# A weights' loader that moves at fixed feature blocks of each token tile, in a kernel of attention and two MLPs

## The chip, the cores and the metric

The kernel runs on one core of one Trainium2 chip. The metric is the device time of one execution in microseconds (us). The kernel before took 1242.02 us (median of 3 runs, 1241.17 to 1243.66).

## The reference

Attention with a learned relative position bias (4 batches, 8 heads, 576 positions, 64 channels a head) gives 2304 tokens of 512 channels. Two MLPs follow, all in float32:

```
x = attention(q, k, v, bias).reshape(2304, 512)
h = x @ w_in                                   # 512 -> 2048
x = (h * clip(h + 3, 0, 6) / 6) @ w_out        # 2048 -> 512
gate = 1 / (1 + exp(-(x @ w_gate)))            # 512 -> 1536
return (gate * (x @ w_val)) @ w_out2           # 1536 -> 512
```

## The kernel before

Bias and attention take the first 361 us or so; the change does not touch them. What follows is called the first part (the first MLP) and the second part (the gated one).

**Tiles and blocks.** The tokens go in 6 token tiles of 384 (TW). The first part walks over its 16 feature blocks of 128 in two halves: eight blocks for all six tiles, then the other eight for all six. The second part does the same with 12 blocks, six a half. "Tile 1" to "tile 12" of a part below are these passes in order; f (first part) and e (second part) are the feature blocks. Float32 products are taken as pairs of high and low parts: a projection of one block is 12 matmuls (L507 to L509), the output projection of one block is 12 matmuls in the first part (L564: high, high, low of the activations) and 9 in the second (L619).

**The chain of a block.** First part: project into PSUM, ScalarE Relu (L513), VectorE product g (L514), ScalarE rounds g to its high part gh (L544), VectorE subtracts for the low part gl (L545), and out1 (L564) uses both two blocks later. Second part: two projections, ScalarE Sigmoid (L633), VectorE product (L634), the same split L544 and L545, and out2 (L619) one block later. At the end of a tile split_x splits the next tile's tokens (ScalarE L499, VectorE L500), and the last blocks' out1 or out2 runs; their blocks' chain is then not covered by projections of the same tile. Sums are taken out of PSUM (L307 on ScalarE, L309 or L602 on VectorE) and stored.

**The loader.** The weights come as 68 tiles of 512 columns in 8-byte numbers that must be turned into float32 and split. One tick() moves three weight tiles on by one stage each: split of tile i-2 (ScalarE cast L149, GpSimd subtraction L150), assemble of tile i-1 (VectorE L139, L141, L143), the DMAs of tiles i and i+1 (SyncE's queue, L125), magnitude of tile i (ScalarE Abs L131, VectorE L132). 28 slots hold finished tiles; a slot comes free when its block's last tile is done. go_on() ticks if a slot is free, and a loop ahead of each block ticks until that block's own weights are there (`while load.done < 2 * f + 2`). In the first part go_on is called at even blocks, and at every block of the first and the last tile of each half; in the second part at every block.

**What sets the order.** The engines run their instructions in the order of their own queues. The tile framework's scheduler sets that order: it does not keep the order of the program text, so a tick's VectorE instructions can stand some blocks away from the place of the call. Nothing in the kernel keeps them out of the last blocks of a tile.

Of the kernel before, what the change touches and what calls it, by code (L numbers as in the profile page):

```python
# [10 lines left out]
F32 = mybir.dt.float32  # L11
F32R = mybir.dt.float32r
I32 = mybir.dt.int32
AF = mybir.ActivationFunctionType
ALU = mybir.AluOpType
# [12 lines left out]
NTILE = NT // TW  # L28
# [65 lines left out]
def block_kernel(ctx: ExitStack, tc: tile.TileContext, q, k, v, mlp, w_in, w_out, w_gate, w_val, w_out2, dist_d,  # L94
                 rows_d, out):
    nc = tc.nc
# [6 lines left out]
    half = keep.tile([P, 1], F32, name="half")  # L103
# [68 lines left out]
    def ring(name):  # L172

        if name == "z":
            return stg.tile([P, 512], F32, name="z", bufs=4)
        return stg.tile([P, 2, 512], F32, name="raw", bufs=2)
# [128 lines left out]
    def evac(eng, dst, src):  # L305
        if eng == "A":
            nc.scalar.copy(dst, src)  # L307
        else:
            nc.vector.tensor_copy(dst, src)  # L309
# [106 lines left out]
    with ExitStack():  # L416
# [55 lines left out]
        pend = None  # L472
        for G in range(S // 16):
# [16 lines left out]
            pend = (G, ps)  # L490
# [6 lines left out]
        def split_x(x):  # L497
            for c in range(4):
                nc.scalar.copy(XH[:, c], x[c])  # L499
                nc.vector.tensor_tensor(out=XL[:, c], in0=x[c], in1=XH[:, c].bitcast(F32), op=ALU.subtract)  # L500

        def project(slot, ps=None):
            ps = mp.tile([P, 512], F32, name="h", bufs=4) if ps is None else ps
            for c in range(4):
                wh = slot[:, 0, P * c : P * c + P]
                wl = slot[:, 1, P * c : P * c + P]
                nc.tensor.matmul(ps[:, 0:TW], wh, XH[:, c], start=(c == 0), stop=False)  # L507
                nc.tensor.matmul(ps[:, 0:TW], wl, XH[:, c], start=False, stop=False)  # L508
                nc.tensor.matmul(ps[:, 0:TW], wh, XL[:, c], start=False, stop=(c == 3))  # L509
            return ps[:, 0:TW]  # L510

        def hardswish(g, ph):
            nc.scalar.activation(g, ph, AF.Relu, bias=half, scale=1.0 / 6.0)  # L513
            nc.vector.scalar_tensor_tensor(out=g, in0=g, scalar=1.0, in1=ph, op0=ALU.min, op1=ALU.mult)  # L514
            return g
# [5 lines left out]
        for i in range(NSLOT):  # L521
# [5 lines left out]
            if i in (NS // 2 + 1, NS // 2 + 2):  # L527
                f = len(begun)
# [9 lines left out]
        mp = ctx.enter_context(tc.tile_pool(name="mp", bufs=1, space=PSUM, reuse_waits="tile"))  # L538
        slots += [moe.tile([P, 2, 512], F32R, name=f"slot{i}") for i in range(NPRE, NALL)]

        def split_g(g):
            gh = moe.tile([P, TW], F32R, name="gh", bufs=3)
            gl = moe.tile([P, TW], F32R, name="gl", bufs=3)
            nc.scalar.copy(gh, g)  # L544
            nc.vector.tensor_tensor(out=gl, in0=g, in1=gh.bitcast(F32), op=ALU.subtract)  # L545
            return gh, gl

        def go_on(freed, to):

            if load.n - 2 < min(NALL + freed, to):  # L550
                load.tick()

        def take(src):
            x = moe.tile([P, 4, TW], F32, name="take", bufs=2)
            nc.sync.dma_start(x, src)
            return x


        def out1(f, g, os, first, last):
            gh, gl = g  # L560
            sl = slots[(2 * f + 1) % NALL]
            for r, x in ((0, gh), (1, gh), (0, gl)):
                for c in range(4):
                    nc.tensor.matmul(os[c][:, 0:TW], sl[:, r, P * c : P * c + P], x,  # L564
                                     start=(first and r == 0 and x is gh), stop=(last and x is gl))

        NH = NF // 2
        todo = [(part2, t) for part2 in range(2) for t in range(NTILE)]
        X2 = None
        for part2, t in todo:  # L570
            os, pend = [], []
            part = take(part_d[t]) if part2 else None
            for f in range(NH * part2, NH * part2 + NH):
                while load.done < 2 * f + 2:
                    load.tick()
                g = begun.pop(f) if f in begun and t == 0 else None
                if g is None:
                    g = hardswish(moe.tile([P, TW], F32, name="g", bufs=2), project(slots[2 * f % NALL]))
                if not os:
                    os += [mp.tile([P, 512], F32, name=f"o{c}") for c in range(4)]  # L580
                pend.append((f, split_g(g), os, f == NH * part2, f == NH * part2 + NH - 1))
                if len(pend) > 2:
                    out1(*pend.pop(0))
                freed = 2 * NH * part2
                if t == NTILE - 1:
                    freed += max(0, 2 * (f - NH * part2 - 1))
                if f % 2 == 0 or t == 0 or t == NTILE - 1:
                    go_on(freed, 68)
            if (part2, t) != todo[-1]:
                u = todo[todo.index((part2, t)) + 1][1]  # L590
                split_x([x[:, TW * u : TW * (u + 1)] for x in x1])
            else:
                X2 = take(x2[0])
                split_x([X2[:, c] for c in range(4)])
                X2 = take(x2[1])
            for args in pend:
                out1(*args)
            for c in range(4):
                if c % 2 == 0:
                    two = ring("raw")  # L600
                if part2:
                    nc.vector.tensor_tensor(out=two[:, c % 2, 0:TW], in0=os[c][:, 0:TW], in1=part[:, c], op=ALU.add)  # L602
                else:
                    evac("AV"[c % 2], two[:, c % 2, 0:TW], os[c][:, 0:TW])
                if c % 2 == 1:
                    nc.sync.dma_start((x2 if part2 else part_d)[t][:, c - 1 : c + 1], two[:, :, 0:TW])
# [7 lines left out]
        def out2(e, g, os, first, end, last):  # L614
            gh, gl = g
            sl = slots[(2 * NF + 3 * e + 2) % NALL]
            mm = [(i, x, r) for x, r in ((gh, 0), (gh, 1), (gl, 0)) for i in range(NB)]
            for i, x, r in sorted(mm, key=lambda m: m[0]) if last else mm:
                nc.tensor.matmul(os[i], x[:, P * i : P * i + P], sl[:, r], start=(first and x is gh and r == 0),  # L619
                                 stop=(end and x is gl))  # L620

        NH = NE // 2
        for j, (part2, t) in enumerate(todo):
            os = [mp.tile([P, 512], F32, name=f"o{c}") for c in range(NB)]
            prev = None
            for e in range(NH * part2, NH * part2 + NH):
                while load.done < 2 * NF + 3 * e + 3:
                    load.tick()
                s0 = 2 * NF + 3 * e
                pg = project(slots[s0 % NALL])  # L630
                pv = project(slots[(s0 + 1) % NALL])
                g = moe.tile([P, TW], F32, name="g", bufs=2)
                nc.scalar.activation(g, pg, AF.Sigmoid)  # L633
                nc.vector.tensor_tensor(out=g, in0=g, in1=pv, op=ALU.mult)  # L634
                gg = split_g(g)
                if prev is not None:
                    out2(e - 1, prev, os, e - 1 == NH * part2, False, False)
                prev = gg
                freed = 2 * NF + 3 * NH * part2
                if t == NTILE - 1:  # L640
                    freed += 3 * (e - NH * part2)
                go_on(freed, 68)
            if j + 1 < len(todo):
                split_x([X2[:, c] for c in range(4)])
                if j + 2 < len(todo):
                    X2 = take(x2[todo[j + 2][1]])
            out2(NH * part2 + NH - 1, prev, os, False, True, j == len(todo) - 1)
            for i in range(NB):
                o = acc[NB * t + i]
                if part2:  # L650
                    nc.vector.tensor_tensor(out=o, in0=o, in1=os[i], op=ALU.add)
                    nc.sync.dma_start(out[TW * t + P * i : TW * t + P * i + P, :], o)
                else:
                    evac("AV"[i % 2], o, os[i])
# [27 lines left out]
```

## Time and profile before

| | before |
|---|---|
| median of 3 runs | 1242.02 us |
| profiled execution: time / span | 1240.27 / 1238.5 us |
| granted TensorE clock, mean | 0.992 |
| TensorE busy | 1197.9 us (97%) |
| VectorE busy | 705.5 us (57%) |
| ScalarE busy | 557.5 us (45%) |
| GpSimd busy | 274.8 us (22%) |
| loader's DMAs (raw) | 68 of 512 KB, 3.5 us from issue to landing |
| L150 (GpSimd, loader) | 68 of 1352 ns |
| L545 (VectorE, gl) | 166 of 623 ns |
| L141, L143 (VectorE, loader) | 68 of 961 ns, 68 of 759 ns |

The span is the profiled execution from its first to its last instruction, and 1.77 us of that execution lie around it. TensorE is busy in nearly all of it, so a change can only win where TensorE waits or where its clock is not granted in full. A mean over the span hides that: the clock of 0.992 is made of long stretches at 1.0 and a few short ones well below.

### The profile page before, as it was taken

Reading aid. Unit: us, or ns where it says so; the run is one execution under the profiler, and the core shown is the slowest. Engines: PE = TensorE matmul, PEld = TensorE weight load, DVE = VectorE, ACT = ScalarE, POOL = GpSimd, SP = SyncE. Lnnn points to the kernel's source line nnn. Section 1 sums busy time; section 2 is a strip of 40 time slices with the busy share of each in tenths; the row PEclk is TensorE's granted clock in tenths of the full one; section 3 lists DMA queues with packets and bytes.
Section 4 is the critical chain, followed back from the end, with each engine's and each line's share of the span. In section 5 each row is a group of like instructions: output and inputs, shape, how many; then the busy total and the mean of one; then the engine's idle time right before and its main releaser. Section 6 shows DMA issues by size and latency. Waiting matters only on the chain.

```text
span 1238.5 us, 18871 instructions
## 1 busy us (share of the span) xinstructions
PE 1197.9 (97%) x7302; PEld 1065.0 (86%) x7302; DVE 705.5 (57%) x1402; ACT 557.5 (45%) x1171; POOL 274.8 (22%) x222
## 2 busy tenths in 40 slices
PE   7899999999998999998999999989999999999998
PEld 3367777776788999998999999979999999999998
DVE  8977787777868765367753338772212532223332
ACT  5878777777754444345433335332212432212221
POOL 4935556655412210031200003210000210000000
PEclk9999999999999999999999999999999999999999
DMA  5652636254213331032411104540000101011000
GB/s 169 231 183 79 200 88 183 87 154 115 90 35 115 118 109 60 26 128 95 152 53 52 44 28 137 175 145 26 26 1 26 60 26 52 4 47 52 26 26 26
DMA packets 36154, 106.78 MB, mean 86 GB/s; under 512 B 3936, under 2 KB 10336, under 8 KB 36064
## 3 DMA queue, kind: packets, MB, share of 16 engines
q1 hardware_dynamic: 36064, 105.57, 26.3%
q8 instruction: 57, 0.93, 0.3%
q14 instruction: 33, 0.27, 0.1%
HBM read 80.78 MB, written 24.77 MB: 85 GB/s over the span
## 4 chain that ended last, share of the span: by engine, by line
PE 79%; DVE 11%; ACT 4%; DMA 3%; issue 3%; POOL 0%; DVEq 0%; ACTq 0%; SPq 0%; POOLq 0%
PE o L564 12%; PE h L509 11%; PE h L507 11%; PE h L508 11%; PE o L619 11%; PE s L259 6%; PE av L349 5%; PE tr L317 4%; DVE z L141 2%; PE s L486 2%; PE av L352 2%; DMA raw<-in_part_dram 1%; DVE z L143 1%; DVE x L481 1%; DVE z L132 1%
## 5 line engine op out<-in xcount | busy, mean ns | idle before, releaser
L507 PE MATMUL h<-early,slot 128*128 128x384 f32 x952 | 319.0, 335 | 0.0
L509 PE MATMUL h<-early,slot 128*128 128x384 f32 x952 | 318.8, 335 | 0.0
L508 PE MATMUL h<-early,slot 128*128 128x384 f32 x952 | 318.4, 334 | 0.0
L150 POOL TENSOR_TENSOR slot<-z,slot 128x512 fp32r<-128x512 f32 x68 | 91.9, 1352 | 617.7 <-ACT slot L149 352.3
L507 PEld LDWEIGHTS h<-early,slot 128*128 128x128 f32 x952 | 179.2, 188 | 2.7
L508 PEld LDWEIGHTS h<-early,slot 128*128 128x128 f32 x952 | 178.8, 188 | 2.6
L509 PEld LDWEIGHTS h<-early,slot 128*128 128x128 f32 x952 | 178.6, 188 | 0.0
L544 ACT CAST gh<-g 128x384 fp32r<-128x384 f32 x166 | 85.1, 513 | 185.9 <-DVE g L634 125.3
L564 PE MATMUL o<-gh,slot 128*128 128x384 f32 x768 | 154.0, 343 | 12.4 <-ACT gh L544 12.4
L634 DVE TENSOR_TENSOR g<-g,h 128x384 f32<-128x384 f32 x72 | 39.8, 553 | 206.2 <-PE h L509 205.1
L564 PEld LDWEIGHTS o<-gh,slot 128*128 128x128 f32 x768 | 137.7, 192 | 15.3 <-ACT gh L544 15.3
L545 DVE TENSOR_TENSOR gl<-g,gh 128x384 fp32r<-128x384 f32 x166 | 103.5, 623 | 71.9 <-ACT gh L544 70.6
L619 PE MATMUL o<-slot,gh 128*128 128x512 f32 x432 | 112.8, 396 | 4.9 <-ACT gh L544 4.9
L279 ACT ACTIVATE p<-u,stat 128x576 f32<-128x576 f32 x128 | 98.6, 772 | 42.0 <-DVE stat L263 37.7
L259 PE MATMUL s<-k,q 128*128 128x288 f32 x640 | 112.4, 310 | 0.3 <-DVE stat L263 0.3
L633 ACT ACTIVATE g<-h 128x384 f32<-128x384 f32 x72 | 35.4, 491 | 170.5 <-PE h L509 170.5
L263 DVE CUSTOM_DVE_ANT_0 u<-s,bias 128x576 f32<-128x576 f32 x128 | 93.5, 752 | 12.9 <-PE s L259 11.1
L619 PEld LDWEIGHTS o<-slot,gh 128*128 128x128 f32 x432 | 80.7, 189 | 18.8 <-ACT gh L544 5.4
L513 ACT ACTIVATE g<-h,half 128x384 f32<-128x384 f32 x94 | 54.3, 577 | 92.8 <-PE h L509 92.7
L514 DVE SCALAR_TENSOR_TENSOR g<-g,h 128x384 f32<-128x384 f32 x94 | 51.7, 550 | 70.9 <-ACT g L513 70.9
L259 PEld LDWEIGHTS s<-k,q 128*128 128x128 f32 x640 | 89.5, 189 | 2.4 <-DVE stat L263 0.7
L564 PE MATMUL o<-gl,slot 128*128 128x384 f32 x384 | 83.9, 340 | 0.0
(95 smaller groups left out, 1609.8 us busy)
## 6 DMA issues: line engine op xcount, KB each, us to landing
raw<-in_part_dram SPq DMA_DIRECT2D x68, 512.0 KB, 3.5
nbias<-p SPq DMA_DIRECT2D x18, 576.0 KB, 4.5
early<-in_part_dram SPq DMA_DIRECT2D x32, 288.0 KB, 4.3
bias<-nbias SPq DMA_DIRECT2D x16, 576.0 KB, 6.4
take<-x SPq DMA_DIRECT2D x12, 768.0 KB, 4.2
vn<-in_part_dram SPq DMA_DIRECT2D x16, 320.0 KB, 3.4
early<-in_part_dram SPq DMA_DIRECT2D x16, 304.0 KB, 3.8
part<-raw SPq DMA_DIRECT2D x12, 384.0 KB, 2.6
```

Source lines behind the costliest of these rows:

```text
L150: nc.gpsimd.tensor_tensor(out=slot[:, 1], in0=z, in1=slot[:, 0].bitcast(F32), op=ALU.subtract)
L259: nc.tensor.matmul(ps[:, a, 0:HS], Q[:, q0 : q0 + P], K[:, r, h, HS * a : HS * a + HS], start=(i == 0), stop=(i == len(mm) - 1))
L263: nc.vector.tensor_tensor_reduce(out=halves(u), in0=ps[:, :, 0:HS], in1=halves(bt), op0=ALU.add, op1=ALU.min, scale=-0.125, scalar=3e38, a ...
L279: nc.scalar.activation(probs(t), us.pop(t), AF.Exp, bias=low[n % 2][:, s : s + 1], scale=-1.0, accum_out=sums[n % 3][:, s : s + 1])
L349: nc.tensor.matmul(ps[64 * h : 64 * h + 64, 0:HS], vt[:, 4 * h + g], ptm[:, h, g, cols], start=(g == 0), stop=False)
L507: nc.tensor.matmul(ps[:, 0:TW], wh, XH[:, c], start=(c == 0), stop=False)
L508: nc.tensor.matmul(ps[:, 0:TW], wl, XH[:, c], start=False, stop=False)
L509: nc.tensor.matmul(ps[:, 0:TW], wh, XL[:, c], start=False, stop=(c == 3))
L544: nc.scalar.copy(gh, g)
L545: nc.vector.tensor_tensor(out=gl, in0=g, in1=gh.bitcast(F32), op=ALU.subtract)
L564: nc.tensor.matmul(os[c][:, 0:TW], sl[:, r, P * c : P * c + P], x, start=(first and r == 0 and x is gh), stop=(last and x is gl))
L619: nc.tensor.matmul(os[i], x[:, P * i : P * i + P], sl[:, r], start=(first and x is gh and r == 0), stop=(end and x is gl))
```

## The change

Three things are changed.

1. The loader's tick is called only at blocks that are not among the last two of a tile (`f % NH < NH - 2`, `e % NH < NH - 2`). In the first part that is at every one of the first six blocks in the very first tile, and at the even ones of the first six in every other tile, the last tiles of a half among them; in the second part at each of the first four blocks of a tile. By the loops, 49 weight tiles have been split when the second part begins, where it was 53.
2. In the first part's very first tile, gl of the first six blocks is subtracted by GpSimd and not by VectorE.
3. Behind the last tile of the first part ScalarE takes the sigmoid of a one-column tile (`half`), whose result nobody reads, so that ScalarE's table for the sigmoid is loaded there and not at the second part's first block.

```
-        def split_g(g):
+        def split_g(g, eng):
             gh = moe.tile([P, TW], F32R, name="gh", bufs=3)
             gl = moe.tile([P, TW], F32R, name="gl", bufs=3)
             nc.scalar.copy(gh, g)
-            nc.vector.tensor_tensor(out=gl, in0=g, in1=gh.bitcast(F32), op=ALU.subtract)
+            eng.tensor_tensor(out=gl, in0=g, in1=gh.bitcast(F32), op=ALU.subtract)
...
-                pend.append((f, split_g(g), os, f == NH * part2, f == NH * part2 + NH - 1))
+                pend.append((f, split_g(g, nc.gpsimd if (part2, t) == (0, 0) and f < NH - 2 else nc.vector), os, f == NH * part2, f == NH * part2 + NH - 1))
...
-                if f % 2 == 0 or t == 0 or t == NTILE - 1:
+                if f % NH < NH - 2 and (f % 2 == 0 or (part2, t) == (0, 0)):
                     go_on(freed, 68)
+            if (part2, t) == todo[-1]:
+                nc.scalar.activation(half, half, AF.Sigmoid)
...
-                gg = split_g(g)
+                gg = split_g(g, nc.vector)
...
-                go_on(freed, 68)
+                if e % NH < NH - 2:
+                    go_on(freed, 68)
```

**What the scheduler makes of it.** GpSimd, in the first part's first tile. The slot_ rows are the loader's subtractions, the gl rows are moved here from VectorE:

```order
 L290 TENSOR_TENSOR spread<-stat,one 128x128 x2
+L545 TENSOR_TENSOR gl<-z,gh 128x384
 L150 TENSOR_TENSOR slot_4233<-z,slot_4233 128x512
+L545 TENSOR_TENSOR gl<-z,gh 128x384
 L150 TENSOR_TENSOR slot_4234<-z,slot_4234 128x512
 L150 TENSOR_TENSOR slot_4235<-z,slot_4235 128x512
+L545 TENSOR_TENSOR gl<-g,gh 128x384
 L150 TENSOR_TENSOR slot_4236<-z,slot_4236 128x512
+L545 TENSOR_TENSOR gl<-g,gh 128x384
 L150 TENSOR_TENSOR slot_4237<-z,slot_4237 128x512
```

GpSimd does about one gl beside each of its loader subtractions. VectorE at the seventh block (f = 6) of the same tile; z_4448 is the weight tile that is assembled last there, g_4451 the seventh block's product. Before:

```order
L132 TENSOR_SCALAR z_4448<-z_4448 128x512
L139 TENSOR_SCALAR z_4448<-z_4448 128x512
L141 SCALAR_TENSOR_TENSOR z_4448<-raw_4404,z_4448 128x512
L514 SCALAR_TENSOR_TENSOR g_4451<-g_4451,h_4452 128x384
L143 SCALAR_TENSOR_TENSOR z_4448<-raw_4404,z_4448 128x512
L545 TENSOR_TENSOR gl_4468<-g_4451,gh_4467 128x384
```

And now:

```order
L132 TENSOR_SCALAR z_4448<-z_4448 128x512
L139 TENSOR_SCALAR z_4448<-z_4448 128x512
L141 SCALAR_TENSOR_TENSOR z_4448<-raw_4404,z_4448 128x512
L143 SCALAR_TENSOR_TENSOR z_4448<-raw_4404,z_4448 128x512
L514 SCALAR_TENSOR_TENSOR g_4451<-g_4451,h_4452 128x384
L545 TENSOR_TENSOR gl_4468<-g_4451,gh_4467 128x384
```

The product of f = 6 stands behind one loader instruction more (L143). Next, VectorE at the end of tile 6 of the first part (the last tile of its first half); early_ is the split of the next tile's tokens. Before:

```order
L132 TENSOR_SCALAR z_6148<-z_6148 128x512
L139 TENSOR_SCALAR z_6148<-z_6148 128x512
L514 SCALAR_TENSOR_TENSOR g_5991<-g_5991,h_5992 128x384
L141 SCALAR_TENSOR_TENSOR z_6148<-raw_6070,z_6148 128x512
L545 TENSOR_TENSOR gl_6008<-g_5991,gh_6007 128x384
L143 SCALAR_TENSOR_TENSOR z_6148<-raw_6070,z_6148 128x512
L500 TENSOR_TENSOR early_4154<-x0_63,early_4154 128x384
L500 TENSOR_TENSOR early_4154<-x1_64,early_4154 128x384
L500 TENSOR_TENSOR early_4154<-x2_65,early_4154 128x384
L514 SCALAR_TENSOR_TENSOR g_6033<-g_6033,h_6034 128x384
```

And now:

```order
L514 SCALAR_TENSOR_TENSOR g_5939<-g_5939,h_5940 128x384
L545 TENSOR_TENSOR gl_5956<-g_5939,gh_5955 128x384
L514 SCALAR_TENSOR_TENSOR g_5971<-g_5971,h_5972 128x384
L545 TENSOR_TENSOR gl_5988<-g_5971,gh_5987 128x384
L500 TENSOR_TENSOR early_4154<-x0_63,early_4154 128x384
L500 TENSOR_TENSOR early_4154<-x1_64,early_4154 128x384
L500 TENSOR_TENSOR early_4154<-x2_65,early_4154 128x384
L500 TENSOR_TENSOR early_4154<-x3_66,early_4154 128x384
L514 SCALAR_TENSOR_TENSOR g_6003<-g_6003,h_6004 128x384
```

No loader instruction (z_) stands between the last three products of that tile any more. Last, VectorE in the second part's first tile, between the products of two neighbouring blocks. Before:

```order
L634 TENSOR_TENSOR g_8129<-g_8129,h_8116 128x384
L545 TENSOR_TENSOR gl_8133<-g_8129,gh_8132 128x384
L132 TENSOR_SCALAR z_8256<-z_8256 128x512
L139 TENSOR_SCALAR z_8256<-z_8256 128x512
L141 SCALAR_TENSOR_TENSOR z_8256<-raw_8202,z_8256 128x512
L143 SCALAR_TENSOR_TENSOR z_8256<-raw_8202,z_8256 128x512
L132 TENSOR_SCALAR z_8324<-z_8324 128x512
L139 TENSOR_SCALAR z_8324<-z_8324 128x512
L141 SCALAR_TENSOR_TENSOR z_8324<-raw_8254,z_8324 128x512
L143 SCALAR_TENSOR_TENSOR z_8324<-raw_8254,z_8324 128x512
L634 TENSOR_TENSOR g_8181<-g_8181,h_8168 128x384
```

And now:

```order
L636 TENSOR_TENSOR g_8090<-g_8090,h_8077 128x384
L545 TENSOR_TENSOR gl_8094<-g_8090,gh_8093 128x384
L132 TENSOR_SCALAR z_8317<-z_8317 128x512
L139 TENSOR_SCALAR z_8317<-z_8317 128x512
L141 SCALAR_TENSOR_TENSOR z_8317<-raw_8263,z_8317 128x512
L143 SCALAR_TENSOR_TENSOR z_8317<-raw_8263,z_8317 128x512
L132 TENSOR_SCALAR z_8369<-z_8369 128x512
L139 TENSOR_SCALAR z_8369<-z_8369 128x512
L141 SCALAR_TENSOR_TENSOR z_8369<-raw_8315,z_8369 128x512
L143 SCALAR_TENSOR_TENSOR z_8369<-raw_8315,z_8369 128x512
L636 TENSOR_TENSOR g_8142<-g_8142,h_8129 128x384
```

The row numbers of the kernel's lines shift by two or three; the order of this stretch is the same, two whole weight tiles between two products. On ScalarE the added sigmoid (L590) stands between the Relu and the rounding to gh of the first part's last block (f = 15).

## Rows read from the trace of the kernel before

**Rows 1.** Waits of TensorE, 355–1240 us: engine line waited for: us total, times, longest.

```profile
PE o L564 <- ACT gh L544: 12.4, 9, 2.9
PE o L619 <- ACT gh L544: 4.9, 1, 4.9
```

**Rows 2.** Chain that ended last, tile ends of both parts: start us, us, what.

```profile
428.96 2.37 PE o L564 x12
...
458.37 6.24 PE o L564 x36
...
524.93 6.24 PE o L564 x36
...
565.85 3.87 PE o L564 x12
...
602.83 3.83 PE o L564 x12
...
733.64 6.24 PE o L564 x36
...
818.00 3.92 PE o L619 x9
...
855.30 4.12 PE o L619 x18
...
892.84 4.12 PE o L619 x18
```

**Rows 3.** TensorE's timeline: start us, us, what, xcount, [idle before <-releaser].

```profile
363.02 1.55 PE L564 MATMUL o<-gh,slot 128*128 128x384 f32 x8
...
388.12 2.82 PE L564 MATMUL o<-gh,slot 128*128 128x384 f32 x8 [2.05 <-ACT gh L544]
...
394.74 0.85 PE L564 MATMUL o<-gl,slot 128*128 128x384 f32 x4
...
776.16 1.42 PE L564 MATMUL o<-gl,slot 128*128 128x384 f32 x4
```

**Rows 4.** Window behind a wait: stretch, us, busy of PE to POOL, PEclk, DMA.

```profile
565.00:570.00 5.00, 4.15 (x15) 4.15 (x16) 1.88 (x5) 1.33 (x3) 0.00 (x0) 0.66 0.02 3
```

**Rows 5.** VectorE's timeline, last product of tile 6, first part.

```profile
564.71 0.54 DVE L514 SCALAR_TENSOR_TENSOR g<-g,h 128x384 f32<-128x384 f32 x1
```

**Rows 6.** Timeline at the end of tile 5, first part, no loader work there.

```profile
525.21 0.58 ACT L513 ACTIVATE g<-h,half 128x384 f32<-128x384 f32 x1
...
526.41 0.51 ACT L544 CAST gh<-g 128x384 fp32r<-128x384 f32 x1 [0.62 <-DVE g L514]
...
528.93 1.55 PE L564 MATMUL o<-gh,slot 128*128 128x384 f32 x8
```

**Rows 7.** GpSimd and VectorE side by side in tile 2, first part.

```profile
411.85 1.49 POOL L150 TENSOR_TENSOR slot<-z,slot 128x512 fp32r<-128x512 f32 x1 [6.41 <-ACT slot L149]
412.22 1.66 DVE L141 SCALAR_TENSOR_TENSOR z<-raw,z 128x512 int32<-128x512 int32 x1
413.81 0.55 DVE L545 TENSOR_TENSOR gl<-g,gh 128x384 fp32r<-128x384 f32 x1
...
418.12 0.68 DVE L141 SCALAR_TENSOR_TENSOR z<-raw,z 128x512 int32<-128x512 int32 x1
```

**Rows 8.** VectorE's timeline, products of the second part, tiles 1 and 2.

```profile
792.39 0.54 DVE L634 TENSOR_TENSOR g<-g,h 128x384 f32<-128x384 f32 x1
...
816.86 0.54 DVE L634 TENSOR_TENSOR g<-g,h 128x384 f32<-128x384 f32 x1
...
830.34 0.55 DVE L634 TENSOR_TENSOR g<-g,h 128x384 f32<-128x384 f32 x1
```

**Rows 9.** ScalarE's timeline at the second part's first block.

```profile
779.75 1.28 ACT L633 ACT_TABLE_LOAD   x1 [3.21 <-PE h L509]
781.04 0.49 ACT L633 ACTIVATE g<-h 128x384 f32<-128x384 f32 x1
```

**Rows 10.** Groups by line, a one-column ACTIVATE | busy, mean ns.

```profile
L430 ACT ACTIVATE stat<-one 128x1 f32<-128x1 f32 x1 | 0.2, 203 | 0.0
```

## The prediction

> **What bounds the kernel now.** I read the busy shares first: TensorE is at work in 1197.9 of 1238.5 us, so only its stalls and its clock can give anything. The waits of TensorE from 355 us on then show whom it waits for in the two MLP parts [rows 1]: out1 (L564) waits nine times for gh, 12.4 us in all, and out2 (L619) once, 4.9 us. The third view, the chain that ended last, says where. With the ends of the tiles taken from it (start plus length), each tile's time can be had and compared with one in which nothing stalls.
>
> Of the first part tile 3 ends at 458.37 + 6.24 = 464.61 and tile 5 at 524.93 + 6.24 = 531.17 [rows 2]. That makes (531.17 - 464.61) / 2 = 33.28 us for a clean tile, or 2.08 for each of its 16 groups of 12 matmuls. In the second part the clean tile is 896.96 - 859.42 = 37.54, or 6.26 a block. What each other tile has above this [rows 2, 3]:
>
> - Tile 1: from 363.02 to 395.59 with 13 groups (27.04) in it, so 5.53 too long. One wait of 2.05 is in it, before the matmuls at 388.12, and the following matmuls run at half clock.
> - Tile 2: 431.33 - 395.59 - 33.28 = 2.46.
> - Tile 6: 569.72 - 531.17 - 33.28 = 5.27. Tile 7: 606.66 - 569.72 - 33.28 = 3.66. Tiles 8 to 11 together: 0.10. Tile 12: 777.58 - 739.88 - 33.28 = 4.42.
> - Second part, tile 1: 821.92 - 777.58 - 37.54 = 6.80. Its tiles 2 and 3 are clean.
>
> A stall costs more than its wait: in the 5 us after that of tile 6 the granted clock is 0.66 [rows 4], TensorE being at the lower of its two levels (1.2 against 2.4 GHz) in most of it, which loses 0.34 x 5 = 1.7 us.
>
> The cause in tiles 2, 6, 7 and 12 is the same: loader instructions stand between the last products on VectorE. In tile 6 the last product starts at 564.71 [rows 5] and the out1 that ends the tile, 3.87 us long at the low clock, can only begin behind it at 565.85 [rows 2]. In the clean tile 5 the Relu of the last block is over at 525.79 and gh is there at 526.92, while TensorE comes for it only at 528.93 [rows 6], 2.0 us later.
>
> **The change part by part.** *The loader out of the last two blocks.* The order of VectorE shows no loader rows between the last products of tile 6, and the same holds at the ends of tiles 2, 7 and 12. A tile without them is tile 5, so I take the whole excess of tiles 2, 6, 7, 8 to 11 and 12 off: 2.46 + 5.27 + 3.66 + 0.10 + 4.42 = 15.9 us. Bounds: none of it is left (-15.9), or half of it stays, if ScalarE's and VectorE's loader work still runs late because it waits in order for its DMA (-8). I take -15.9, since the order, not a duration, removes the cause.
>
> *What is carried into the second part.* Four weight tiles fewer are done when it begins (49 against 53). VectorE does two of them between products: from 792.39 to 816.86 are three blocks [rows 8], 8.16 a block, so 4.08 a weight tile, against the 6.26 that TensorE needs. So VectorE falls back 1.90 a block. In tile 1 the order is unchanged, two whole weight tiles between products, so its 6.80 stays: 0. In tile 2 the four further weight tiles come before the products of the third to fifth block. Before, the second block's product is at 830.34 [rows 8], when nothing is late; two further blocks at 1.90 make it 3.8 late, and TensorE wants a block's gh only one block (6.26) after its projections, less 1.13 for product and rounding (526.92 - 525.79, [rows 6]). 3.8 is under 5.1, so 0; if it were all exposed, 4 x 4.08 = 16.3.
>
> *gl on GpSimd in the first tile.* Six subtractions of 0.55 us leave VectorE [rows 7]: -3.3. But GpSimd and VectorE hinder each other: L141 takes 1.66 us when it starts while GpSimd subtracts (from 411.85 on), and 0.68 when it doesn't [rows 7], so 0.98 more for a GpSimd instruction of 512 columns. For 384 columns I estimate 0.98 x 384 / 512 = 0.73, and six of them give +4.4. The seventh block's product stands behind L143 as well now, an instruction about as long as the free L141: +0.7. Sum: -3.3 + 4.4 + 0.7 = +1.8, since VectorE is what the wait at 388.12 hangs on. Bounds: -5.5, if the stall of tile 1 goes altogether (none of the six GpSimd rows meets a VectorE instruction that it hinders), and 6 x 0.98 + 0.7 - 3.3 = +3.3. I take +1.8, the value nearest to the row of a hindered instruction, as VectorE has hardly a gap in this tile.
>
> The Trainium skill has a rule that speaks against this edit ("SBUF — State Buffer", section "Who interferes with whom"): a VectorE instruction with two inputs in SBUF and a GpSimd instruction that reads SBUF lock each other out of a shared port pair for a whole instruction. The pair 1.66 and 0.68 agrees with it; without such a lock the edit would be worth -3.3 + 0.7 = -2.6 instead of +1.8.
>
> *The sigmoid's table.* It is loaded at 779.75 for 1.28 us now, with ScalarE idle for 3.21 us before it [rows 9], so its removal there gives nothing. Where it goes, ScalarE loads it between Relu and the rounding of the last block, in which it waits 0.62 for the product anyhow. Load and a one-column ACTIVATE of 0.20 [rows 10] are 1.48, less 0.62 is 0.9 later: gh at 527.8 on the times of tile 5, and TensorE comes at 528.93. So 0, with 1.1 us to spare. If that cover were gone it would be 0.9 plus some 1.7 of clock.
>
> By the Trainium skill ("ScalarE: Activation LUTs", section "What ACT_TABLE_LOAD costs") a switch is a load of 1283 ns and a drain of 1380 ns, 2.66 us. With this gh comes 0.2 us too late, and the sum is 0.2 to 2 us worse, still within the forecast's own range below. The trace shows 1.28 for the load, and the sigmoid at 781.04 begins at once behind it, so the drain isn't seen here.
>
> *Sum.* -15.9 + 1.8 + 0 + 0 = -14.1 us on the profiled execution: its span 1238.5 becomes 1224.4, and with the 1.77 around it the execution 1226.2. The median of the runs is 1.75 above the profiled execution, so the time is 1227.9, say 1228.
>
> **The rivals.** *A, the second part's stall goes too.* The sigmoid table is out of tile 1, and with fewer weight tiles in flight at its start the products could come earlier: -14.1 - 6.8, 1221.1. Against it: the order on VectorE between the products is the same, and 8.16 a block does not change.
>
> *B, the first tile recovers.* GpSimd's subtractions fall into gaps, and the stall at 388.12 goes: -5.5 in place of +1.8, 1220.6. For it: 3.3 us leave the engine that is waited for. Against it: 1.66 against 0.68.
>
> *C, half of the gain at the ends.* The ticks are called earlier, but the loader's steps wait for their DMA and run in the last blocks all the same, or the waits move to blocks five and six: -8 + 1.8, about 1236. Against it: a wait needs to last some 2 us at a block that has no cover, and blocks before the last two have 5.1.
>
> *D, slower: the debt comes due.* The loader's lag shows in the second part's tile 2. If the four weight tiles run with nothing beside them (16.3) and a half clock (1.7) follows, it is -14.1 + 18 = +4, so 1246. It decides from the point at which 14.1 us of it are exposed. Against it: the lag of 3.8 us at the fourth block lies below 5.1.
>
> **How the numbers follow.** Forecast 0.68 (own range 1224 to 1232), A 0.09, B 0.10, C 0.07, D 0.06. The range reaches from 1219.5, under A and B, to 1234, short of C and D. A difference below 0.2%, 2.5 us, can't be told from none here. Faster is the forecast, A, B and most of C: 0.91. Within 0.2% is the upper tail of C and the lower one of D: 0.03. Slower is D: 0.06.
>
> **What would show it.** TensorE's waits for gh at L564 should fall from 12.4 to about 2 to 4 us, all in tile 1; tiles 2 to 12 should each take 33.3 us. The wait at L619 should stay at 4.9, and the second part's tile 2 should stay at 37.5. L141 or L143 at 1.4 us or more should be seen about six times more in tile 1. The table load should stand near the last block of the first part, with no wait of TensorE behind it. The forecast is wrong if a tile other than these two still takes over 34 us in the first part, or if a wait at L619 shows in tile 2.

## The result and the profile after

The changed kernel took 1229.55 us (median of 4 runs, 1228.21 to 1231.55) against 1241.78 for the kernel before in the same comparison (4 runs): ratio 0.990, 95% interval 0.988 to 0.992, so 12.2 us less. The forecast was 1228, 14.1 us less. In a later comparison (e8 below) the same kernel took 1232.15 us (10 runs) against 1240.87 (17), so 8.7 us less: its gain is less sure than the first interval says.

The waits of TensorE for gh from 355 us on (engine line waited for: us in all, times, longest) answer to [rows 1]:

```profile
PE o L621 <- ACT gh L544: 5.3, 1, 5.3
PE o L564 <- ACT gh L544: 5.3, 3, 3.6
```

L621 is the old L619. The first part's waits fell from 12.4 to 5.3 us, in three places, all in tile 1 (2 to 4 us had been expected there); the second part's one wait stayed, at 5.3 in place of 4.9. The chain that ended last (start us, us, what) at the ends of tiles 1 to 6 and 12 of the first part and 1 and 2 of the second, against [rows 2]:

```profile
397.53 2.35 PE o L564 x12
...
426.92 6.24 PE o L564 x36
...
460.20 6.24 PE o L564 x36
...
526.76 6.24 PE o L564 x36
...
560.04 6.24 PE o L564 x36
...
759.72 5.73 PE o L564 x33
...
806.72 4.21 PE o L621 x9
...
845.01 4.12 PE o L621 x18
```

Tile 1 ends at 399.88, tile 2 at 433.16: 33.28. Tile 12's last row ends at 765.45 and holds 33 of its last 36 matmuls; counted from the first to the last tile's matmuls, each of tiles 2 to 12 takes 33.28. The excess that they had, 15.8 us by the same count, is gone altogether.

TensorE in tile 1 (start us, us, what, [idle before <-releaser]), against [rows 3]:

```profile
386.64 1.66 PE L564 MATMUL o<-gh,slot 128*128 128x384 f32 x8 [0.58 <-ACT gh L544]
...
392.62 2.93 PE L564 MATMUL o<-gh,slot 128*128 128x384 f32 x8 [3.62 <-ACT gh L544]
...
397.53 1.66 PE L564 MATMUL o<-gh,slot 128*128 128x384 f32 x8 [1.06 <-ACT gh L544]
399.03 0.85 PE L564 MATMUL o<-gl,slot 128*128 128x384 f32 x4
```

All three waits of the first part are here. The tile begins at 365.09 in this profile and lasts to 399.88, 7.75 longer than its 13 groups; before it was 5.53. In the profile before, tile 1 had a second wait beside the one of 2.05 that the prediction names, and tile 2 began with a third:

```profile
393.22 1.68 PE L564 MATMUL o<-gh,slot 128*128 128x384 f32 x8 [1.20 <-ACT gh L544]
...
402.95 1.68 PE L564 MATMUL o<-gh,slot 128*128 128x384 f32 x8 [1.11 <-ACT gh L544]
```

The account of the two profiled spans, 1238.5 and 1228.2: +2.1 until tile 1 begins (363.02 to 365.09), +2.2 in tile 1, -15.8 in tiles 2 to 12, +1.2 in the first two tiles of the second part. Together -10.3.

The loader's work on VectorE shows where the excess went. Weight tiles assembled (L141) in tiles 1 to 12 of the first part: 8, 5, 4, 2, 0, 6, 8, 2, 0, 0, 0, 6 before and 7, 3, 3, 3, 3, 2, 3, 3, 3, 3, 2, 2 after. Loader instructions between the last three products of each tile: 8, 1, 0, 0, 0, 8, 9, 0, 0, 0, 0, 7 before; after, none but the 8 of tile 1, which keeps its stall.

### The profile page after: what moved, and what is told of

It is laid out like the page before. It is cut to its first block, busy times and chain, and to the rows that moved or that the text cites. A ratio compares the mean times of both kernels' runs of the same rounds, so it can differ in the third digit from the quotient of the medians.

```text
span 1228.2 us, 18857 instructions
## 1 busy us (share of the span) xinstructions
PE 1193.3 (97%) x7302; PEld 1061.6 (86%) x7302; DVE 705.3 (57%) x1396; ACT 560.1 (46%) x1172; POOL 280.2 (23%) x228
## 4 chain that ended last, share of the span: by engine, by line
PE 86%; DVE 7%; ACT 3%; issue 2%; DMA 1%; POOL 0%; DVEq 0%; ACTq 0%; SPq 0%; POOLq 0%
PE o L564 15%; PE h L507 12%; PE h L509 12%; PE h L508 12%; PE o L621 11%; PE s L259 6%; PE av L349 5%; PE tr L317 4%; PE s L486 2%; PE av L352 2%; DVE z L141 1%; DVE x L481 1%; DVE z L132 1%; DVE z L143 1%; PE tr L296 1%
## 5 line engine op out<-in xcount | busy, mean ns | idle before, releaser
L507 PE MATMUL h<-early,slot 128*128 128x384 f32 x952 | 319.2, 335 | 0.0
L150 POOL TENSOR_TENSOR slot<-z,slot 128x512 fp32r<-128x512 f32 x68 | 91.1, 1340 | 588.0 <-ACT slot L149 431.5
L507 PEld LDWEIGHTS h<-early,slot 128*128 128x128 f32 x952 | 179.0, 188 | 2.7
L564 PE MATMUL o<-gh,slot 128*128 128x384 f32 x768 | 150.2, 336 | 5.3 <-ACT gh L544 5.3
L545 DVE TENSOR_TENSOR gl<-g,gh 128x384 fp32r<-128x384 f32 x162 | 102.1, 630 | 72.6 <-ACT gh L544 71.5
L564 PEld LDWEIGHTS o<-gh,slot 128*128 128x128 f32 x768 | 135.4, 189 | 6.2 <-ACT gh L544 6.2
L621 PE MATMUL o<-slot,gh 128*128 128x512 f32 x432 | 113.0, 397 | 5.3 <-ACT gh L544 5.3
L263 DVE CUSTOM_DVE_ANT_0 u<-s,bias 128x576 f32<-128x576 f32 x128 | 93.5, 753 | 14.5 <-PE s L259 11.9
L621 PEld LDWEIGHTS o<-slot,gh 128*128 128x128 f32 x432 | 80.9, 189 | 19.2 <-ACT gh L544 5.7
L564 PE MATMUL o<-gl,slot 128*128 128x384 f32 x384 | 82.3, 335 | 0.0
```

The lines of the kernel that those rows point to most:

```text
L150: nc.gpsimd.tensor_tensor(out=slot[:, 1], in0=z, in1=slot[:, 0].bitcast(F32), op=ALU.subtract)
L263: nc.vector.tensor_tensor_reduce(out=halves(u), in0=ps[:, :, 0:HS], in1=halves(bt), op0=ALU.add, op1=ALU.min, scale=-0.125, scalar=3e38, a ...
L545: eng.tensor_tensor(out=gl, in0=g, in1=gh.bitcast(F32), op=ALU.subtract)
```

## Experiments

In the table each kernel's excess is what a tile took above 27.04 (tile 1) or 33.28 us in the first part and 37.54 in the second, counted from matmul starts in its one profile. Each ratio is to the runs of the kernel before in the same comparison (medians 1241.78 for the changed kernel, 1241.71 for e1 to e4, 1240.87 for e5 to e8). "Start" is the first out1 (L564).

| kernel | median us (runs) | ratio to before, 95% | start | tile 1 | tile 2 | tiles 3 to 12 | second part, tiles 1 + 2 |
|---|---|---|---|---|---|---|---|
| before | 1241.78 (4) | | 363.0 | 5.4 | 2.5 | 13.3 | 6.7 + 0.2 |
| changed | 1229.55 (4) | 0.990 (0.988 to 0.992) | 365.1 | 7.6 | 0 | 0 | 7.2 + 0.9 |
| e1: gl on VectorE | 1229.06 (6) | 0.990 (0.987 to 0.992) | 364.8 | 6.3 | 0 | 0 | 7.5 + 0.7 |
| e2: ticks only | 1226.54 (6) | 0.988 (0.985 to 0.992) | 372.4 | 5.0 | 0 | 0 | 6.9 + 1.1 |
| e3: gl on GpSimd only | 1243.23 (12) | 1.001 (1.000 to 1.003) | 365.0 | 9.4 | 0.4 | 12.9 | 7.1 + 0.1 |
| e4: early table only | 1242.60 (12) | 1.000 (0.998 to 1.002) | 363.9 | 6.7 | 1.2 | 13.4 | 7.2 + 0.2 |
| e5: ticks behind their block | 1224.02 (5) | 0.985 (0.983 to 0.988) | 366.8 | 7.6 | 0 | 0 | 0.4 + 0 |
| e6: loader's subtractions on VectorE | 1221.90 (6) | 0.985 (0.981 to 0.988) | 374.0 | 0 | 0 | 0 | 7.1 + 0.1 |
| e7: both | 1213.95 (6) | 0.978 (0.976 to 0.981) | 362.4 | 0 | 0 | 0 | 0.4 + 0 |
| e8: changed, again | 1232.15 (10) | 0.993 (0.991 to 0.995) | 365.4 | 9.3 | 0.1 | 0 | 7.1 + 1.1 |

The theory at this point: the ticks' places take away the excess of tiles 2 to 12, GpSimd's gl makes tile 1 longer because GpSimd's subtractions hold VectorE up, the early table does nothing, and the second part's stall is VectorE's rate of two weight tiles a block.

**e1, gl back on VectorE.**

```
-  pend.append((f, split_g(g, nc.gpsimd if (part2, t) == (0, 0) and f < NH - 2 else nc.vector), os, ...
+  pend.append((f, split_g(g, nc.vector), os, ...
```

> The changed kernel with gl of the first tile back on VectorE. Theory (GpSimd's subtractions hold up VectorE): tile 1 goes from 7.75 us too long back to about 5.5, all other tiles stay, so 2.2 us less than the changed kernel, about 1227.3. Rival (the longer first tile has another cause, and the move takes 3.3 us off VectorE): tile 1 stays at 7.7 or grows to 11, 1229.5 to 1233.

Tile 1 is 6.3 too long, not 5.5, and below the changed kernel's 7.6. The medians, 1229.06 (1227.3 had been expected) and 1229.55, do not tell the two apart; TensorE's waits in the tile do, 4.4 against 5.3 us, with the others below.

**e2, the ticks' places alone** (e1 without the early sigmoid).

```
-            if (part2, t) == todo[-1]:
-                nc.scalar.activation(half, half, AF.Sigmoid)
```

> The kernel before with the new places of the ticks alone: no gl on GpSimd, no early sigmoid table. Theory (the table costs and gives nothing): the same as with gl on VectorE and the early table, about 1227.3; tiles 2 to 12 at 33.28 each, the second part's first tile at 44.3 to 44.7. Rival (the early table helps the second part's first tile, or hurts the last tile of the first part): 1.3 to 2.7 us apart from that kernel, in one of these two tiles.

Tiles 2 to 12 are clean without the two other edits. Against e1, the second part's first two tiles take 8.0 and 8.2: the table is worth nothing. The median is 2.5 us below e1's, with overlapping intervals (its six runs go from 1224.50 to 1234.71), and no tile of the second part shows such a gain. Tile 1 differs by 1.3 from e1 with the same code in it, and that is the clock: TensorE waits 4.4 us there in e1 and 4.5 in e2, but behind nearly the same longest wait its matmuls run slowly in e1,

```profile
394.69 2.93 PE L564 MATMUL o<-gh,slot 128*128 128x384 f32 x8 [2.74 <-ACT gh L544]
```

and at full speed in e2:

```profile
402.28 1.68 PE L564 MATMUL o<-gh,slot 128*128 128x384 f32 x8 [2.77 <-ACT gh L544]
```

In the 5 us from there on the granted clock is 0.71 in e1 and 1.00 in e2.

**e3, gl on GpSimd alone.**

```
-            nc.vector.tensor_tensor(out=gl, in0=g, in1=gh.bitcast(F32), op=ALU.subtract)
+            eng.tensor_tensor(out=gl, in0=g, in1=gh.bitcast(F32), op=ALU.subtract)
...
+  pend.append((f, split_g(g, nc.gpsimd if (part2, t) == (0, 0) and f < NH - 2 else nc.vector), os, ...
```

> The kernel before with gl of the first tile's first six blocks on GpSimd, nothing else. Theory: tile 1 from 5.5 to about 7.7 us too long, 1241.8 + 2.2 = 1244.0. Rival (the move relieves VectorE): tile 1 at 0 to 3 us too long, 1236 to 1239.5.

Tiles 1 and 2 together are 9.8 too long, against 7.8 in each of the two kernels with the ticks of before (before and e4): +2.0. The time is 1.5 us up with an interval that includes 1. So the rival, that the move relieves tile 1, falls. With the new ticks the tile's excess is 7.6, 7.6 and 9.3 with gl on GpSimd (changed, e5, e8) and 6.3 and 5.0 without (e1, e2): 2.5 apart in the mean. But these figures mix waits with the clock behind them, which e1 and e2 have just shown to differ for the same code. Taken apart (us; tiles 1 and 2 together, the clock that of tile 1):

| kernel | gl of tile 1 on | excess | TensorE's waits | longest wait | the rest | granted clock |
|---|---|---|---|---|---|---|
| before | VectorE | 7.8 | 5.1 | 2.0 | 2.7 | 0.95 |
| e4 | VectorE | 7.8 | 4.4 | 2.7 | 3.4 | 0.93 |
| e1 | VectorE | 6.3 | 4.4 | 2.7 | 1.9 | 0.95 |
| e2 | VectorE | 5.0 | 4.5 | 2.8 | 0.6 | 1.00 |
| e3 | GpSimd | 9.8 | 5.0 | 3.6 | 4.8 | 0.87 |
| changed | GpSimd | 7.6 | 5.3 | 3.6 | 2.3 | 0.95 |
| e5 | GpSimd | 7.6 | 5.2 | 3.6 | 2.4 | 0.95 |
| e8 | GpSimd | 9.4 | 4.9 | 3.6 | 4.5 | 0.86 |

The longest wait is 3.6 in each of the four kernels with gl on GpSimd and 2.8 or less in the others. With the new ticks the waits together are 0.7 longer in the mean; with the old ones they are 5.0 with the move and 4.4 and 5.1 (there in four pieces) without. So the move costs TensorE 0.7 us of waiting in the changed kernel. The rest, 0.6 to 4.8 us, goes with the clock, and whether the longer wait is why it is larger with the move is not shown.

VectorE by line in tile 1 (365.1 to 399.9) of the changed kernel, shapes x count | busy us, mean ns | idle before:

```profile
L141 DVE SCALAR_TENSOR_TENSOR z<-raw,z 128x512 int32<-128x512 int32 x7 | 8.8, 1261 | 0.2
L143 DVE SCALAR_TENSOR_TENSOR z<-raw,z 128x512 int32<-128x512 int32 x7 | 7.1, 1011 | 0.2
L139 DVE TENSOR_SCALAR z<-z 128x512 int32<-128x512 int32 x7 | 4.3, 621 | 0.1
L132 DVE TENSOR_SCALAR z<-z 128x512 f32<-128x512 f32 x7 | 4.2, 593 | 3.9 <-ACT z L131 3.9
...
L545 DVE TENSOR_TENSOR gl<-g,gh 128x384 fp32r<-128x384 f32 x2 | 1.9, 940 | 0.6 <-ACT gh L544 0.6
```

The same in e1 (364.8 to 398.2), where the same seven weight tiles are made:

```profile
L141 DVE SCALAR_TENSOR_TENSOR z<-raw,z 128x512 int32<-128x512 int32 x7 | 7.6, 1090 | 0.1
L143 DVE SCALAR_TENSOR_TENSOR z<-raw,z 128x512 int32<-128x512 int32 x7 | 4.8, 682 | 0.0
L132 DVE TENSOR_SCALAR z<-z 128x512 f32<-128x512 f32 x7 | 4.6, 663 | 1.3 <-ACT z L131 1.3
L545 DVE TENSOR_TENSOR gl<-g,gh 128x384 fp32r<-128x384 f32 x6 | 4.1, 682 | 0.6 <-ACT gh L544 0.6
...
L139 DVE TENSOR_SCALAR z<-z 128x512 int32<-128x512 int32 x7 | 3.0, 425 | 0.2
...
L545 DVE TENSOR_TENSOR gl<-z,gh 128x384 fp32r<-128x384 f32 x1 | 1.7, 1661 | 0.0
```

The loader's instructions cost VectorE 24.4 us in the one and 20.0 in the other. So they take 4.4 more with gl on GpSimd, and L143 shows it best: 1011 against 682 ns. gl itself takes 3.9 less (1.9 against 4.1 + 1.7, of which the last begins ahead of the tile). VectorE also waits 2.6 us longer for ScalarE's L131: 1.41 up to 365.05 and 1.21 up to 375.31, two places where in e1 it subtracts gl (from 363.30 and 373.73 on). So not all of the time that gl leaves free is won.

**e4, the early table alone.**

```
+            if (part2, t) == todo[-1]:
+                nc.scalar.activation(half, half, AF.Sigmoid)
```

> The kernel before with the early sigmoid table, nothing else. Here the last block of tile 12 has no cover, since loader work holds up its product and TensorE waits for its gh. Theory: the table load stands in that wait, tile 12 from 4.4 to 5.3 us too long, and nothing comes back at the second part's start: 1242.7. Rival (the load at the second part's first block was on the path): tile 1 of the second part 1.3 us or more shorter, 1240.5 or less.

Time and tiles are those of before within what varies: nothing is gained at the second part's start, and tile 12 is not longer either (4.1 against 4.3). That cost was forecast too high: the timeline of ScalarE and VectorE at the end of tile 12 shows gh late, but only by the part of the load that the product does not cover.

```profile
772.88 1.28 ACT L590 ACT_TABLE_LOAD   x1
772.98 0.55 DVE L514 SCALAR_TENSOR_TENSOR g<-g,h 128x384 f32<-128x384 f32 x1
774.18 0.20 ACT L590 ACTIVATE half<-half 128x1 f32<-128x1 f32 x1
774.29 0.49 ACT L544 CAST gh<-g 128x384 fp32r<-128x384 f32 x1
```

The product there is over at 773.53 (772.98 + 0.55), so gh begins 0.8 late; TensorE waits 2.6 at that place, where it was 2.0, and a wait of 0.3 before it is gone.

**e5, one weight tile a block in the second part.**

```
-                nc.scalar.activation(g, pg, AF.Sigmoid)
-                nc.vector.tensor_tensor(out=g, in0=g, in1=pv, op=ALU.mult)
+                sig = nc.scalar.activation(g, pg, AF.Sigmoid)
+                mul = nc.vector.tensor_tensor(out=g, in0=g, in1=pv, op=ALU.mult)
...
                 if e % NH < NH - 2:
-                    go_on(freed, 68)
+                    with tc.issue_after(mul.ins), tc.issue_after(sig.ins):
+                        go_on(freed, 68)
```

issue_after only sets the order: what the tick issues on VectorE and ScalarE is queued behind that block's product and Sigmoid.

> The changed kernel with each tick of the second part queued behind its own block's Sigmoid and product on ScalarE and VectorE, so that one weight tile and not two stands between two products. Theory (VectorE's 8.16 us a block against 6.26 makes the second part's stall): one weight tile makes 4.1 + 1.1 = 5.2 a block, the waits at out2 go, tiles 1 and 2 of the second part lose 7.20 + 0.91 = 8.1 us: 1221.4. Rival (the stall hangs on something else, such as the weights' DMAs or the split of the next tile's tokens at the tile's end): at least 5 us of it stay, 1226 or more.

The median, 1224.02, is 2.6 above what was expected, but the changed kernel ran at 1232.15 in the same comparison (e8): 8.1 us more, the amount that was forecast for this edit. The waits at out2 are gone, and what is left of TensorE's waits for gh from 355 us on is tile 1's:

```profile
PE o L564 <- ACT gh L544: 5.2, 3, 3.6
```

VectorE between the third and the fourth product of the second part's first tile, in e5:

```profile
782.81 0.55 DVE L636 TENSOR_TENSOR g<-g,h 128x384 f32<-128x384 f32 x1 [2.59 <-PE h L509]
...
784.87 0.69 DVE L141 SCALAR_TENSOR_TENSOR z<-raw,z 128x512 int32<-128x512 int32 x1
...
789.89 0.54 DVE L636 TENSOR_TENSOR g<-g,h 128x384 f32<-128x384 f32 x1
```

One L141 stands there, where there were two (8.16 us a block, [rows 8]), and VectorE has idle time before the product. The second part's 8.1 us fall to 0.4.

**e6, the loader's subtractions on VectorE in tile 1** (e1, and L150 of that tile's ticks on VectorE; GpSimd is left with two subtractions at the tile's end, from 392.75 and 397.99 on).

```
-                nc.gpsimd.tensor_tensor(out=slot[:, 1], in0=z, in1=slot[:, 0].bitcast(F32), op=ALU.subtract)
+                self.eng.tensor_tensor(out=slot[:, 1], in0=z, in1=slot[:, 0].bitcast(F32), op=ALU.subtract)
...
-            os, pend = [], []
+            os, pend, load.eng = [], [], nc.vector if (part2, t) == (0, 0) else nc.gpsimd
```

> As the kernel with gl of the first tile on VectorE, but in that tile the loader's subtractions run on VectorE too, so that GpSimd does nothing beside it. Theory (a GpSimd subtraction holds VectorE up by 0.98 us, more than the 0.69 that it costs on VectorE): six of them save 6 x 0.3 = 1.8 us, tile 1 from 5.0 to 6.3 (two profiles) to about 4. Rival (no such hold-up): VectorE gets 6 x 0.69 = 4.1 more, tile 1 at about 10.

Tile 1's excess does not fall to 4 but to nothing. VectorE by line in that tile (374.0 to 401.0):

```profile
L141 DVE SCALAR_TENSOR_TENSOR z<-raw,z 128x512 int32<-128x512 int32 x7 | 5.8, 825 | 0.1
...
L143 DVE SCALAR_TENSOR_TENSOR z<-raw,z 128x512 int32<-128x512 int32 x6 | 4.1, 684 | 0.1
L150 DVE TENSOR_TENSOR slot<-z,slot 128x512 fp32r<-128x512 f32 x5 | 3.4, 687 | 0.4 <-ACT slot L149 0.2
...
L139 DVE TENSOR_SCALAR z<-z 128x512 int32<-128x512 int32 x7 | 3.0, 422 | 0.1
L132 DVE TENSOR_SCALAR z<-z 128x512 f32<-128x512 f32 x7 | 2.9, 421 | 0.0
```

Five subtractions cost VectorE 3.4 us here, and L141 and L132 alone are 3.5 shorter than in e1; gl of the first block is 0.55 where it was 1.66, and the splits of the tokens 0.54 where they were 0.75. So VectorE does five instructions more in less time. The window is shorter, and one L143 fewer lies in it. The loader's instructions between the last products of tile 1 are still there (8, as in e1), but none of them is held up, and no wait is left: neither the two waits nor the low clock behind them. The rival is refuted. The one slow L141 of the seven (1.67 us, from 399.37 on; the others take 0.68 to 0.69) runs when GpSimd subtracts again.

**e7, both** (e5's and e6's edits together).

> The ticks of the second part queued behind their own block, and in the first tile of the first part both gl and the loader's subtractions on VectorE. Theory: the second part's 8.1 us go and tile 1 falls to about 4: 1229.1 - 8.2 - 1.8 = 1219. Rival: the first tile gets longer (10), 1225.

1213.95 us, 18.2 less than the changed kernel's 1232.15 and 26.9 less than the 1240.87 of before, both in the same comparison. It was expected at 1219: tile 1 fell to nothing and not to 4. TensorE waits nowhere for gh, and the granted clock is full (stretch, us, busy of PE, PEld, DVE, ACT, POOL, PEclk, DMA, GB/s; tile 1, and from there to the last tile of the first part):

```profile
362.40:389.50 27.10, 27.10 (x159) 27.10 (x158) 26.39 (x49) 15.44 (x29) 3.98 (x2) 1.00 0.29 98
389.50:750.00 360.50, 360.50 (x2081) 360.50 (x2080) 207.88 (x365) 154.12 (x288) 37.62 (x28) 1.00 0.24 84
```

This is the version that beats both. VectorE is busy for 26.4 of the 27.1 us of tile 1, so there is next to nothing to spare there.

**e8, the changed kernel again.**

> The changed kernel once more, for what varies between runs. Theory: the part up to the first out1 (363 to 372 us in six profiles) varies from run to run whatever the kernel; tile 1 at 7.2 to 8.0 us too long again, tiles 2 to 12 at 33.28, the second part's first two tiles at 7.7 to 8.5 together; 1226 to 1232. Rival (the 2.07 us more ahead of tile 1 belong to the change): 365 us again.

Two of its figures miss what was expected: tile 1 is 9.3 too long and not 7.2 to 8.0 (its waits are no longer, the clock is lower), and the median, 1232.15, lies at the edge of 1226 to 1232. The start is at 365 again, so this pair does not refute the rival; e1, e2, e5 and e6 start at 364.8 to 374.0, e7 at 362.4, e3 and e4 at 365.0 and 363.9. The late ones, e2 and e6, have one wait of 12 us in the bias stage, for ScalarE's L479, which the change does not touch; each of the two profiles is of the slowest run of its kernel. Without these two the four kernels with gl on GpSimd start at 365.0 to 366.8 and the four others at 362.4 to 364.8. But the difference is there before any edited instruction runs: the first projection (L507) starts at 353.51 before and at 355.58 in the changed kernel, 9.5 us ahead of out1 in every profile, and the first gl on GpSimd at 363.30. Up to that projection TensorE, VectorE and ScalarE have the same instructions in the same order in all ten. What moves the start is not shown, nor why one wait grows to 12 us.

## Why the prediction was right

*The loader out of the last two blocks: -15.9 forecast, -15.8 measured.* e2 shows it as an edit on its own: its time is 15.2 us below before, and tiles 2 to 12 are clean in all seven profiles with the new places but for 0.1 in one, where the three with the old ones have 15.8, 13.3 and 14.5 us too much. For tiles 6, 7 and 12 the cause is as named: 7 to 9 loader instructions stood between the last three products, and none does now. The number of weight tiles fell there too, from 6 to 8 a tile to 2 or 3; tile 3 before, clean with four weight tiles and none of their instructions between its last products, speaks for the place and against the number, but no run moved the places alone with six to eight in a tile. For tile 2 the cause named does not hold. VectorE at its end before:

```profile
424.33 0.55 DVE L514 SCALAR_TENSOR_TENSOR g<-g,h 128x384 f32<-128x384 f32 x1 [0.63 <-ACT g L513]
425.46 0.56 DVE L545 TENSOR_TENSOR gl<-g,gh 128x384 fp32r<-128x384 f32 x1 [0.58 <-ACT gh L544]
425.94 1.96 DVE L500 TENSOR_TENSOR early<-x,early 128x384 fp32r<-128x384 f32 x4
427.81 0.55 DVE L514 SCALAR_TENSOR_TENSOR g<-g,h 128x384 f32<-128x384 f32 x1
```

The last product has the token splits ahead of it and no loader instruction. Of the tile's 2.5 us, 1.1 is the wait at its first block (402.95) and 0.8 one at its end; in e3 and e4, with the same ticks, the tile has no wait at all and is 0.4 and 1.2 us too long, with the clock still low from tile 1. So 2.5 of the 15.9 came off for another reason than the one given, which no run isolates.

*gl on GpSimd: +1.8 forecast; +0.7 in waits, 2.0 to 2.5 with the clock.* The sign was right, and so was the cause: the loader's instructions on VectorE are held up, 4.4 longer (24.4 against 20.0), as sized. L545 gave back 3.9 and not 3.3, since gl itself is held up now and then (1.66 us for one of them in e1). But the hold-up is not made of about six more long L141 and L143: there are 7 of 1.38 us or more in tile 1 against 4 before and 3 in e1, and L139 (621 against 425 ns) pays too. VectorE's time is also not TensorE's: of what the sum took as waiting, TensorE's waits show 0.7, and the rest of the tile's growth is clock, which the sum does not hold. The 0.7 for the L143 ahead of the seventh product cannot be told apart. So the agreement of +1.8 with the +2.2 between two profiles (tile 1 alone; tiles 1 and 2 together are 7.8 too long before and 7.6 after), or with the +2.0 of e3, is luck in its size.

The rule of the Trainium skill that was weighed ("SBUF — State Buffer", section "Who interferes with whom") agrees with e6: with GpSimd out of most of the tile the two-input L141 goes from 1090 to 825 ns in the mean. The single-input L132 goes from 663 to 421 as well, and the Trainium skill allows for that where such an instruction runs in a two-port mode; whether it does here, no run shows.

*The sigmoid's table: 0 forecast, 0 measured* (e4 and e2). In the changed kernel the load hides where it was said to hide:

```profile
760.00 0.57 ACT L513 ACTIVATE g<-h,half 128x384 f32<-128x384 f32 x1
760.60 1.28 ACT L590 ACT_TABLE_LOAD   x1
761.89 0.20 ACT L590 ACTIVATE half<-half 128x1 f32<-128x1 f32 x1
762.00 0.50 ACT L544 CAST gh<-g 128x384 fp32r<-128x384 f32 x1
```

gh is there at 762.50, and TensorE comes for it at 763.72, 1.2 later (forecast 1.1). The drain of 1380 ns that the Trainium skill states ("ScalarE: Activation LUTs", section "What ACT_TABLE_LOAD costs") does not show: the ACTIVATE begins 0.01 us behind the load, as in [rows 9].

*The second part: 0 forecast, +1.2 measured.* This is a term that was mis-sized. Its cause as named held: two weight tiles between two products, and e5 takes the stall away by the order alone. In the changed kernel the wait is 5.3 instead of 4.9, and the rest is clock. The two stretches from the end of the wait on, of the changed kernel:

```profile
806.00:811.00 5.00, 4.28 (x10) 3.42 (x11) 4.93 (x9) 2.34 (x5) 1.27 (x1) 0.50 0.49 170
811.00:816.00 5.00, 5.00 (x27) 5.00 (x27) 1.55 (x4) 2.21 (x4) 1.28 (x1) 0.87 0.58 198
```

and of e6, which has the same ticks and the same stall:

```profile
807.00:812.00 5.00, 4.09 (x11) 3.31 (x12) 4.93 (x9) 2.29 (x4) 1.28 (x1) 0.53 0.53 173
812.00:817.00 5.00, 5.00 (x30) 5.00 (x29) 2.40 (x5) 2.50 (x5) 1.30 (x1) 1.00 0.53 196
```

In the changed kernel TensorE is still at the lower level in the second stretch (0.87), in e6 it is not. By the granted clock it lasts 3.8 us from the end of the wait before, 5.6 after, and 3.7 to 6.1 in the six other profiles that have this stall. So the forecast's 1.7 us for a low clock was one draw: in the second part the excess of the two tiles, less the wait, is 1.9 to 3.0. With the new ticks it was long in four of five profiles and with the old ones in none of three; whether that is chance or comes from the slightly longer wait stays open. The four weight tiles that are owed cost nothing in tile 2: no wait of TensorE is there, as reckoned.

*Ahead of tile 1: nothing forecast, +2.1 in the profiles.* It is there before the first edited instruction runs, and its cause stays open. The medians, in which it is mixed, moved by 12.2, and by 8.7 in e8's comparison.

So the forecast was right in its main term and in the sign and cause of the GpSimd move. It is 1.6 us below the first median and 4.2 below the second: it holds nothing for the longer low clock of tile 1 and of the second part, and that it came as near as 1.6 is in part luck. None of the rivals came about: A and B only became true in e5 and e6, by other edits than the one made, nothing of C's half is left at the ends, and D's debt shows no wait (the 0.9 of the second part's tile 2 is clock).

## What to carry to other kernels

Where an in-order engine makes both the chain that TensorE waits for and background work, look at the order in the last blocks of each tile first: that is where nothing covers the chain, and moving the background work forward cost little elsewhere. Calling the background work less often does not thin it out if a scheduler pulls it forward; queueing it behind a named instruction does (8 us). And taking a subtraction off a busy VectorE to GpSimd can cost more than it frees: 3.9 us freed and 4.4 lost on VectorE here, while the loader's subtractions, moved the other way, took the 5 to 6 us of stall away. And when two profiles differ in a stalled stretch, take its waits and its granted clock apart first: here the same code and the same waits gave 1.3 us of difference by the clock alone.

## What the runs showed of the hardware that was not expected

A GpSimd subtraction of 512 columns (1.3 us) beside a busy VectorE costs it more than doing the subtraction itself (0.69 us): with five of them moved, the lines of VectorE's work in tile 1 add up to 29.4 us (e6) instead of 32.0 (e1, without its one copy out of PSUM; 0.7 of the difference is the L143 that e6's window lacks). After a wait of about 5 us TensorE's low clock lasted anywhere from 3.7 to 6.1 us in eight profiles of nearly the same stall. After a wait of 2.7 or 2.8 us in the same code the clock fell in one profile (e1, 0.71 in the next 5 us) and not in another (e2, 1.00).
